# RWKV-6 attention and an MLP-mixer block on one core: unit 2's own gram moved into the state products' banks, its state products into mixing's banks, unit 3 started later

## The chip, the cores and the metric

The kernel runs on one core of a Trainium2 chip. The metric is the device time of one execution in microseconds; the median of three runs is 534.33 us (533.35 to 536.37). Five engines work beside each other and keep to their own order: TensorE (PE: matmuls, and PEld: its weight loads), VectorE (DVE), ScalarE (ACT), GpSimd (POOL) and SyncE (SP), which here issues nearly all DMAs. They wait for each other by semaphores.

## What is computed

Two blocks follow each other, in float32, for 4 batches, 768 tokens and 8 heads of 48:

```python
for t in range(S):                       # RWKV-6: a state of 48 x 48 per head
    cur = einsum('bhd,bhe->bhde', u * kt, vt)
    y[:, :, t] = einsum('bhd,bhde->bhe', rt, state + cur)
    state = wt[:, :, :, None] * state + einsum('bhd,bhe->bhde', kt, vt)
x = y.transpose(0, 2, 1, 3).reshape(B, S, H * D)
h = relu(x.T @ w_tok1) @ w_tok2          # mixing over tokens
u = x + h.T
out = u + relu(u @ w_ch1) @ w_ch2        # mixing over channels
```

The mixer's four weights come as 64-bit floats and are converted on the chip.

## The kernel before

**Units.** Attention is worked in units of 256 tokens of one batch: three to a batch, twelve in all. "Unit 0" to "unit 2" are the first batch, unit 3 is the first of the second batch. A unit has two blocks of 128 tokens and each of these two chunks of 64; within a chunk the recurrence becomes matmuls. `unit(i)` (L340) returns the steps of one unit as functions:

- `own_u` (four pieces): ScalarE multiplies the keys by u. `own_gram`: 64 small matmuls of these with the queries, `own_put`: VectorE puts their diagonal into the unit's attention matrix `at` (two of these, used in turn).
- `ends` and `begins`: VectorE scans the decays backwards and forwards; `keys` and `queries` multiply them in. `ranges`: two checks on ScalarE of the size of the decays.
- `tokens`: TensorE turns the keys; `copied`: two ScalarE copies of that out of PSUM into `kT`.
- `gram`, `mask`: keys by queries, and VectorE puts the part above the diagonal into `at`.
- `carry`: the products of keys and values that go into the state (`outer`, tile `kv_ps`). `updates`: state = scaled state + product, on VectorE. `scaled`: the state times the decay of a chunk, tile `before`; four ScalarE instructions for each chunk (L432), one for every pair of heads.
- `before`: the queries times the scaled states (`y_ps`, L311); `seen`: a small ScalarE copy that orders what follows; `after`: the attention matrix times the values (L332); `taken`: three ScalarE copies of the result to `x`.

**PSUM banks.** [...] `ps_a` has one tile of two banks, tag "a", for the state products. During the first batch `ps_g` has two tiles of two banks for grams and y, and `ps_m` has two single banks, tag "m", for turned keys and mixing. After the first batch `ps_g` and `ps_m` are closed and `ps_m` has six banks. A tile that takes a buffer waits until the last reader of the tile before it there is done.

**Weight conversions.** `convert` (L189) makes seven steps for each pair of weight pieces: a load by SP, then on VectorE L203 (exponent), L209 (mantissa), L215 (add), L218 (product) and two of L221 (put); on ScalarE L206 (power of two, needs L203) and L212 (sign). L218 needs both. Raw data lies in `scratch` and `spare` in turn. There are three for the token weights (`to_tok`) and nine for the channel weights (`to_ch`; in the text, conversion 0 to 8).

**Order.** `strict` (L88) fixes the order of instructions on TensorE, VectorE and ScalarE to that of the calls. For the first batch's attention the list is written by hand (L716 to L725), with the mixing of batch 0 (`h`) and the first conversions in it. From then on a list of (cost, step) pairs of the attention of the next batch (`steps`, L685) is woven by cost into the pieces of the mixing of the present batch (`woven`, L46). In mixing, `up` (L531) is three matmul instructions and a relu on ScalarE, `down` (L601) the second channel product. What stands in `ahead` (L765) is issued before any step of the next batch. A matmul instruction in float32 is recorded as two.

SP's order is the scheduler's, from the same calls; a load that waits holds those behind it.

## Time and profile before

| | us |
|---|---|
| median of the runs | 534.33 |
| profiled execution | 533.83 |
| its span | 532.0 |
| TensorE busy in the span | 504.4 |
| VectorE busy | 330.7 |
| ScalarE busy | 213.0 |
| PE idle before its first matmul | 8.52 |
| 64 small matmuls of a gram, slow clock / full clock | 1.98 / 1.16 |
| scan over a unit's decays (VectorE) | 2.33 |
| four scaled states of a chunk (ScalarE) | 1.01 |
| update of a state (VectorE) | 0.35 |

The span runs from the first instruction to the last; around it lie 1.83 us of the execution. In the lines of a profile, "x32" counts instructions as recorded, and a bracket names the time that the engine stood idle before a row and what it waited for.

### The profile page before, as it was taken

To read this page: it belongs to the slowest core of one execution; us is meant where nothing else is said; L and a number is where in the kernel's file an instruction comes from. 1 tells how busy PE (TensorE), PEld (TensorE's weight loads), DVE (VectorE), ACT (ScalarE), POOL (GpSimd) and SP (SyncE) were. 2 spreads that over 40 slices of the span, in tenths; PEclk is the share of its full clock that TensorE was granted. 3 is DMA by queue.
4 is the path that set the end of the run, shared out by engine and by line. 5 is a ranking of instruction groups with operands and counts; after the bars stand their busy time and mean duration, and the time that the engine had idled before them with its cause. 6 is when DMAs were issued, how large, how long until landed. Compare 5 with 4: busy or idle time off the path is not lost.

```text
span 532.0 us, 12569 instructions
## 1 busy us (share of the span) xinstructions
PE 504.4 (95%) x5506; PEld 430.1 (81%) x5506; DVE 330.7 (62%) x505; ACT 213.0 (40%) x533; POOL 1.3 (0%) x10
## 2 busy tenths in 40 slices
PE   3669989999999999999999999999999999999997
PEld 3567568766689868898998967898998968999996
DVE  7996899796195654193482665195393625775654
ACT  3857685772242234433343234423424303441400
POOL 0000000000000000000000000000000000000000
PEclk9688999999999999999999999999999999999999
DMA  8967747624222213214212203102000000000000
GB/s 300 331 174 216 225 157 244 190 91 125 95 71 90 91 34 97 60 36 126 60 71 91 64 27 102 31 1 91 1 31 1 3 30 1 1 0 32 1 33 32
DMA packets 20941, 46.01 MB, mean 86 GB/s; under 512 B 2128, under 2 KB 13008, under 8 KB 20880
## 3 DMA queue, kind: packets, MB, share of 16 engines
q1 hardware_dynamic: 20736, 45.14, 26.5%
q8 instruction: 45, 0.74, 0.6%
q14 instruction: 16, 0.13, 0.1%
q10 hardware_dynamic: 144, 0.00, 0.0%
HBM read 40.41 MB, written 4.72 MB: 85 GB/s over the span
## 4 chain that ended last, share of the span: by engine, by line
PE 82%; DVE 12%; ACT 3%; issue 2%; DMA 1%; DVEq 0%
PE q_ps L625 26%; PE z_ps L536 23%; PE h_ps L607 6%; PE z_ps L568 6%; PE h_ps L513 6%; PE h_ps L520 5%; PE y_ps L332 2%; PE y_ps L311 2%; PE kv_ps L297 2%; DVE to_end L366 2%; PE gram L251 2%; PE k_ps L281 1%; PE xT_ps L528 1%; DVE w L374 1%; DVE wch L221 1%
## 5 line engine op out<-in xcount | busy, mean ns | idle before, releaser
L536 PE MATMUL z_ps<-xT,wch 128*128 128x256 f32 x648 | 147.4, 382 | 1.0 <-DVE wch L221 1.0
L536 PEld LDWEIGHTS z_ps<-xT,wch 128*128 128x128 f32 x648 | 120.7, 190 | 17.9 <-DVE wch L221 1.4
L625 PE MATMUL q_ps<-wch,z 128*128 128x192 f32 x444 | 78.5, 328 | 0.0
L625 PEld LDWEIGHTS q_ps<-wch,z 128*128 128x128 f32 x444 | 72.6, 190 | 0.8 <-DVE z L667 0.3
L538 ACT ACTIVATE z<-z_ps 128x256 f32<-128x256 f32 x108 | 41.0, 382 | 79.5 <-PE z_ps L536 78.9
L432 ACT ACTIVATE before<-state,to_end 112x48 f32<-112x48 f32 x176 | 44.2, 324 | 30.3 <-DVE state L442 26.0
L625 PE MATMUL q_ps<-scratch,z 128*128 128x192 f32 x288 | 50.4, 328 | 0.0
L625 PEld LDWEIGHTS q_ps<-scratch,z 128*128 128x128 f32 x288 | 47.0, 190 | 0.3
L442 DVE TENSOR_TENSOR state<-before,kv_ps 112x192 f32<-112x192 f32 x40 | 13.9, 348 | 39.7 <-ACT before L432 31.4
L520 PE MATMUL h_ps<-h,wtok 128*128 128x384 f32 x96 | 34.9, 490 | 0.6 <-ACT h L515 0.6
L607 PE MATMUL h_ps<-wch,z 128*128 128x384 f32 x96 | 32.4, 490 | 0.0
L513 PE MATMUL h_ps<-x,wtok 128*128 128x384 f32 x96 | 32.1, 490 | 0.0
L635 DVE TENSOR_TENSOR o<-x,z 128x192 f32<-128x192 f32 x7 | 2.5, 358 | 45.3 <-ACT z L634 45.3
L522 DVE TENSOR_TENSOR x<-x,h_ps 128x384 f32<-128x384 f32 x24 | 13.3, 553 | 27.4 <-PE h_ps L520 27.3
L366 DVE TENSOR_TENSOR_SCAN to_end<-w,starts 112x1041 f32<-112x1041 f32 (+1 forms) x13 | 28.1, 2159 | 2.0 <-DMA w<-in_w_dram 1.6
L374 DVE TENSOR_TENSOR_SCAN w<-w,starts 112x1041 f32<-112x1041 f32 x12 | 27.9, 2321 | 0.0
L513 PEld LDWEIGHTS h_ps<-x,wtok 128*128 128x128 f32 x96 | 18.2, 192 | 11.6
L607 PEld LDWEIGHTS h_ps<-wch,z 128*128 128x128 f32 x96 | 17.8, 190 | 11.4
L338 ACT COPY x<-y_ps 64x384 f32<-64x384 f32 (+1 forms) x36 | 17.1, 475 | 22.0 <-PE y_ps L332 21.6
L520 PEld LDWEIGHTS h_ps<-h,wtok 128*128 128x128 f32 x96 | 16.6, 190 | 9.4 <-ACT h L515 2.3
L358 ACT ACTIVATE junk<-to_end,least 112x1041 uint8<-112x1041 f32 x12 | 13.9, 1162 | 25.5 <-DVE to_end L366 25.5
L529 ACT COPY xT<-xT_ps 128x384 f32<-128x384 f32 x24 | 11.4, 478 | 23.9 <-PE xT_ps L528 23.8
(140 smaller groups left out, 669.6 us busy)
## 6 DMA issues: line engine op xcount, KB each, us to landing
rk<-in_rk_dram SPq DMA_DIRECT2D x36, 192.0 KB, 3.6
near<-in_near_dram SPq DMA_DIRECT2D x8, 768.0 KB, 4.4
w<-in_w_dram SPq DMA_DIRECT2D x11, 520.5 KB, 3.7
spare<-in_w_ch_dram SPq DMA_DIRECT2D x10, 512.0 KB, 4.3
vt<-in_v_dram SPq DMA_DIRECT2D x12, 384.0 KB, 4.0
out_dram<-o SPq DMA_DIRECT2D x24, 192.0 KB, 1.9
scratch<-in_w_ch_dram SPq DMA_DIRECT2D x8, 512.0 KB, 4.2
rk<-in_rk_dram SPq DMA_DIRECT2D x6, 512.0 KB, 8.4
```

The lines of the kernel that those rows point to most:

```text
L338: return [lambda: act.copy(x[:, 0], got[0])] + [lambda n=n: act.copy(x[ts(n, P), 1], got[1][ts(1 - n, P)]) for n in range(2)]
L358: act.activation(junk[:ROWS], L["to_end"][:ROWS], AF.Relu, bias=bias[:ROWS], scale=scale, accum_out=flags[:ROWS, i, n:n + 1])
L366: dve.tensor_tensor_scan(to, of, start, 0.0, op0=ALU.mult, op1=ALU.add)
L374: dve.tensor_tensor_scan(w_[:ROWS], w_[:ROWS], starts[:ROWS], 0.0, op0=ALU.mult, op1=ALU.add)
L432: act.mul(t[:ROWS, a], state[bt, g][:ROWS, a], by_last(c, j)[:, a:a + 1])
L513: pe.matmul(sums[i], wtok1[:, c, ts(i, 128)], x_of()[:, c, :], start=(c == 0), stop=(c == C - 1))
L520: pe.matmul(ps, wtok2[:, i, ts(c, 128)], h1[:, i, :], start=(i == 0), stop=(i == DTOK // 128 - 1))
L536: pe.matmul(ps, wch1[:, m, ts(jt, 128)], xT[:, m, ts(s, SEG)], start=(m == 0), stop=(m == DM // 128 - 1))
L538: act.activation(zs[s][:, jt, :], ps, AF.Relu)
L568: pe.matmul(ps[:, q], lefts[r][:, ts(q, 128)], of[r], start=first and q == 0, stop=end and q == JB - 1, skip_group_check=True)
L607: pe.matmul(ps, zs[s][:, jt, ts(n, 128)], wch2[:, jt, :], start=(jt == 0), stop=(jt == NJ - 1))
L625: pe.matmul(ps, a[:, j, :], b[:, j, :], start=(j == 0), stop=(j == HJ - 1))
```

## The change

- `grams` takes an optional pool and tag. In unit 2 its own gram takes the two banks of `ps_a`, where the state products of unit 0 were, and not a tile of `ps_g`. In the order by hand it now comes before unit 0's `after`; `own_put` of unit 2 follows that of unit 1, ahead of unit 1's state products.
- `outer` takes `apart`. In unit 2 the products of even and odd chunks lie in two single banks of `ps_m` in place of the tile of `ps_a`.
- In unit 2 the last three `scaled` steps are one VectorE product each in place of four ScalarE instructions.
- The order by hand is changed accordingly: unit 2's `own_u`, `carry` and updates move, and four of the mixing's matmuls come behind unit 2's `before`.
- In unit 3 an empty step of cost 2.0 stands before `tokens`; and the first quarter of the pieces of batch 0's mixing after `ahead` (ups and conversions 2 and 3) is issued before any step of unit 3.

```diff
-    def grams(k_, r_):
+    def grams(k_, r_, where=None):
 
-        both = ps_g and ps_g.tile([128, 2, 512], f32, name="gram")
-        g = [both[:, q] for q in range(2)] if ps_g else [bank("gram") for q in range(2)]
+        where = where or (ps_g and (ps_g, "gram"))
+        both = where and where[0].tile([128, 2, 512], f32, name="gram", tag=where[1])
+        g = [both[:, q] for q in range(2)] if where else [bank("gram") for q in range(2)]
...
-    def outer(kT, vt, half):
+    def outer(kT, vt, half, apart=False):
 
-        kv = ps_a.tile([128, 2, 512], f32, name="kv_ps", tag="a")
+        both = None if apart else ps_a.tile([128, 2, 512], f32, name="kv_ps", tag="a")
+        kv = [bank("kv_ps") if apart else both[:, j] for j in range(2)]
...
         def own_gram():
-            L["own"] = grams(L.pop("uk"), r_)
+            L["own"] = grams(L.pop("uk"), r_, (ps_a, "a") if i == UB - 1 else None)
...
         def carry():
-            L["kv"] = outer(L.pop("kT"), vs[i], half)
+            L["kv"] = outer(L.pop("kT"), vs[i], half, apart=i == UB - 1)
...
                 t = L["before"][g] = apool.tile([128, A, D], f32, name="before", bufs=5)
+                if i == UB - 1 and (c, j) != (0, 0):
+                    return dve.tensor_mul(t[:ROWS], state[bt, g][:ROWS], by_last(c, j).unsqueeze(2).to_broadcast([ROWS, A, D]))
                 for a in range(A):
...
-                (2.4, e["ends"]), (1.2, e["keys"]), (0.4, e["ranges"][0]), (2.2, e["begins"]), (1.0, e["tokens"]), (0.2, e["copied"][0]),
+                (2.4, e["ends"]), (1.2, e["keys"]), (0.4, e["ranges"][0]), (2.2, e["begins"]),
+                *([] if by_tokens else [(2.0, lambda: None)]), (1.0, e["tokens"]), (0.2, e["copied"][0]),
...
-           x0, p0, s0[1], t0[2], m0, g0, e1["begins"], s0[2], t0[3], add0, s0[3], t1[0], e0["before"], e0["seen"], put0, load2,
-           e1["keys"], e0["after"], *e2["own_u"], e1["tokens"], *e1["copied"], e1["queries"], e1["own_put"], e1["carry"], *e0["taken"],
-           lambda: load_v(2), e1["gram"], e2["ends"], s1[0], t1[1], e2["keys"], e2["tokens"], s1[1], t1[2], e2["own_gram"], *e2["copied"],
-           e2["begins"], s1[2], t1[3], e1["mask"], s1[3], t2[0], e2["carry"], e1["before"], e2["queries"], s2[0], t2[1], e1["seen"],
-           e1["after"], e2["own_put"], e2["gram"], s2[1], t2[2], x1, e1["taken"][0], m1, *h[:2], s2[2], t2[3], e1["taken"][1], p1, e2["mask"],
-           e1["taken"][2], s2[3], e2["before"], e2["seen"], add1, g1, put1, to_ch[0][0], e2["after"], *h[2:8], x2, m2, *e2["taken"], p2,
-           add2, g2, *h[8:], put2,
+           x0, p0, s0[1], t0[2], m0, g0, e1["begins"], e2["own_u"][0], s0[2], t0[3], *e2["own_u"][1:], add0, s0[3], e0["before"], e0["seen"],
+           t1[0], e2["own_gram"], put0, load2, e1["keys"], e0["after"], e1["tokens"], *e1["copied"], e1["queries"], e1["own_put"],
+           e2["own_put"], e1["carry"], *e0["taken"], lambda: load_v(2), e1["gram"], e2["ends"], s1[0], t1[1], e2["keys"], e2["tokens"],
+           s1[1], t1[2], *e2["copied"], e2["carry"], e2["begins"], s1[2], t1[3], e1["mask"], s1[3], t2[0], e1["before"], e2["queries"],
+           e1["seen"], e1["after"], e2["gram"], x1, p1, s2[0], t2[1], s2[1], t2[2], s2[2], t2[3], *e1["taken"], s2[3], e2["before"], m1,
+           g1, e2["mask"], e2["seen"], *h[:2], e2["after"], add1, put1, to_ch[0][0], *h[2:8], *e2["taken"], x2, p2, m2, add2, g2, *h[8:], put2,
...
-            pieces = woven(both, sum(to_ch[2:8], [])) + woven(downs[0][:6], to_ch[8]) + downs[0][6:] + downs[1][:8]
+            pieces = woven(both, sum(to_ch[2:8], []))
+            alone = len(pieces) // 4
+            ahead += pieces[:alone]
+            pieces = pieces[alone:] + woven(downs[0][:6], to_ch[8]) + downs[0][6:] + downs[1][:8]
```

In the list, e0 to e2 are the units' steps, s their updates, t their scaled states, and x, m, p, add, g, put the steps of the token weights' conversions. In the built program this gives, on TensorE, 36 matmul instructions of `up` before unit 3's turned keys where 15 stood; on VectorE, conversions 2 and 3 as a whole before unit 3's `ends`; and on SP, the load of `near` and of `u_rows` later among the loads of conversions 5 to 8, in front of conversion 8's.

More of the change, by code (lines that the diff above doesn't have):

```diff
@@ L253, in grams @@
                 start=True, stop=True))
-        if ps_g:
+        if where:
             return [(slice(0, 2), both.rearrange("p q (x t) -> p q x t", x=X))]
@@ L296, in outer @@
                     if 2 * (half * UC + c) + j < 2 * C - 1:
-                        pe.matmul(kv[ts(q, P), j, ds((c * A + a) * D, D)], kT[ts(j, T), c, a, ts(q, P)],
+                        pe.matmul(kv[j][ts(q, P), ds((c * A + a) * D, D)], kT[ts(j, T), c, a, ts(q, P)],
                                   vt[ts(j, T), c, ts(2 * a + q, D)], start=True, stop=True)
@@ L437, in update @@
                 new = state[bt, g + 1] = apool.tile([128, A, D], f32, name="state", bufs=3)
-                got = L["kv"][:ROWS, j, ds(c * A * D, A * D)].rearrange("p (a e) -> p a e", a=A)
+                got = L["kv"][j][:ROWS, ds(c * A * D, A * D)].rearrange("p (a e) -> p a e", a=A)
                 if g == 0:
@@ L838, in by_halves @@
                         new = states[g + 1] = apool.tile([128, A, D], f32, name="before", bufs=5)
-                        got = kv[:ROWS, j, ds(c * A * D, A * D)].rearrange("p (a e) -> p a e", a=A)
+                        got = kv[j][:ROWS, ds(c * A * D, A * D)].rearrange("p (a e) -> p a e", a=A)
                         if g == 0:
```

## The prediction

> **What bounds the kernel now.** I read the page first: busy shares, then the forty slices (13.3 us each).

> ```profile
> PE 504.4 (95%) x5506; PEld 430.1 (81%) x5506; DVE 330.7 (62%) x505; ACT 213.0 (40%) x533; POOL 1.3 (0%) x10
> ...
> PE   3669989999999999999999999999999999999997
> ...
> PEclk9688999999999999999999999999999999999999
> ```

> TensorE is full from the eighth slice on, with a low clock only in the second to fourth. Then busy time by stretch (second column length, third TensorE, then weight loads, VectorE, ScalarE):

> ```profile
> 9.00:110.00 101.00, 85.96 (x1469) 69.28 (x1463) 88.15 (x120) 71.45 (x162) 0.00 (x0) 0.92 0.72 232
> 110.00:200.00 90.00, 90.00 (x894) 66.09 (x893) 56.46 (x73) 30.33 (x80) 0.00 (x0) 1.00 0.24 76
> ```

> TensorE idles 101.00 - 85.96 = 15.04 us between 9 and 110 us, and next to nothing afterwards until the end. The change touches only the work before 140 us and removes no matmul. So the new time is the old one, less idle or slow-clock time removed, plus idle time added, all before about 120 us. The list of waits says what TensorE stood for:

> ```profile
> PE y_ps L311 <- ACT before L432: 2.7, 2, 1.4
> PE gram L251 <- issue: 2.0, 1, 2.0
> PE kv_ps L297 <- DVE state L442: 2.0, 1, 2.0
> PE k_ps L281 <- issue: 2.0, 1, 2.0
> PE y_ps L332 <- ACT seen L320: 1.6, 3, 1.0
> ...
> PE k_ps L281 <- DVE rk L371: 1.0, 1, 1.0
> ```

> The change aims at the 2.0 of kv (at 36.86 us), the 1.0 of k_ps (76.21) and half of the 2.7 of y (1.30 at 99.89). The k_ps "issue" ends at 32.69, just when VectorE's keys of unit 2 end (31.38 + 1.21), so it is really a wait for VectorE. Last, ScalarE's and VectorE's timelines at 70 us, which carry my forecast:

> ```profile
> 71.40 0.38 ACT L538 ACTIVATE z<-z_ps 128x256 f32<-128x256 f32 x1
> 71.68 1.14 ACT L206 ACTIVATE scratch<-scratch,rebias 128x1024 uint16<-128x1024 uint16 x1
> 72.72 1.16 ACT L358 ACTIVATE junk<-to_end,least 112x1041 uint8<-112x1041 f32 x1
> ...
> 73.87 1.17 ACT L212 ACTIVATE scratch<-spare 128x1024 bf16<-128x1024 int32 x1
> ```

> ```profile
> 70.60 2.33 DVE L366 TENSOR_TENSOR_SCAN to_end<-w,starts 112x1041 f32<-112x1041 f32 x1
> ...
> 74.94 1.22 DVE L371 TENSOR_TENSOR rk<-rk,to_end 112x1024 f32<-112x1024 f32 x1
> 76.07 0.68 DVE L218 TENSOR_TENSOR scratch<-scratch 128x1024 bf16<-128x1024 bf16 x1
> ```

> A weight conversion needs ScalarE twice (L206, L212) before VectorE can go on (L218). Unit 3's scan and keys now fill VectorE while ScalarE does that. The change moves exactly this filling away.

> [...] a gram of 64 matmuls takes 1.98 us at 8.52 and 1.16 us at 78.53, and the changes between slow and fast lie near 14.6, 28.2 and 45.3 us. [...] I price the new 112x192 products by L442's 0.35 us of the same size.

> **The change part by part, units 0 to 2.** Times are those of the profiled execution; I follow the built order of the changed program on each engine and what each wait names.
> - Unit 0's y ends at 23.34 (22.21 + 1.13). Unit 2's own gram now follows. Its four scaled keys (4 in 1.70 us) come one before and three behind the third scaled state, which ends at 22.84, so the last is ready at about 24.1; 40 of 64 matmuls remain, at 1.98/64 each 1.2 us: end 25.3. "seen" is ready at 24.2 as before, so within starts at 25.3 instead of 24.36: +0.95.
> - Unit 2's own_put (1.13 us pitch) goes ahead of its scan on VectorE. The gram sat in the state products' banks, so unit 1's kv waits for that: 28.5 + 1.15 = 29.7 instead of 28.13. Behind it wait unit 1's gram and updates; those wait for the same scan anyway. Keys of unit 2 end at 33.7 instead of 32.6.
> - k_ps then ends at 34.8, ScalarE's two copies at 36.05, and unit 2's kv starts at once in mixing's banks; with the old banks it would wait for unit 1's last update at 37.9.
> - Unit 1's "seen" comes behind the first scaled state of unit 2 (37.9 to 38.9): within starts at 39.15 (before 40.78).
> - Unit 2's updates and three products on VectorE take 6 x 0.35 after 39.65: done at 41.85 instead of ScalarE's 44.1. Each product replaces four ScalarE instructions of 0.32.
> - Unit 2's y then waits only for unit 1's results to be taken (1.45 us of copies): with a full clock it ends at 43.3, four matmuls of the mixing at 44.65, within at 45.8. With the slow clock kept until 45.3 (within 1.96, gram 1.95) within ends at 48.1.
> Before, the twenty mixing matmuls that follow start at 48.78. So the gain is 0.75 to 3.0; I take S = 1.8, since 31.7 to 35.1 is still half idle and the slow clock likely comes back.

> **Units 3 on.** Here I keep the clock of before and subtract S at the end, as the whole loop from 50 to 70 us is unchanged and moves along. TensorE now does twelve ups (36 matmul instructions) before k_ps instead of five: an up is 6 recorded matmuls of 0.2265 (5.45/24), 1.36 us. The second ends at 71.15, the twelfth at 84.75.
> - Conversion 2: VectorE is ready at 72.3, but L206, the range check and L212 run 71.68 to 74.9. It ends at 76.9 (0.72 + 1.21).
> - Conversion 3: L203 to 77.5, L206 to 78.55, now the scaled keys of unit 3 (1.6) and one relu (0.3), L212 to 81.55; end 83.5. VectorE stood idle about 2.6 + 2.2 us.
> - Only then unit 3's scan (2.64 with reciprocal) and keys (1.13): 87.3. k_ps waits 84.75 to 87.3: 2.55.
> - Its own gram needs the bank of up 10, whose relu stands behind the next L206 and L212: 87.3 + 0.6 + 1.05 + 0.3 + 1.05 + 0.3 = 90.6; TensorE is there at 89.7: 0.9. A later up waits 0.2 the same way.
> - Scaled-state chain: conversion 5 and own_put end at 97.6, queries 100.7, first update 103.4, ScalarE product to 104.35, L212 to 105.4, conversion 6 to 107.35, mask to 111.3, third update 111.65, L206 and L212 before the third scaled state: 112.55 to 113.5.
> - TensorE has done its 24 ups by 109.0; y waits 1.1 for a bank and then about 2.2 for that state; it ends at 113.9.
> Before, y ended at 100.89 after 54 instructions; 18 more make 18 x 2 x 0.2265 = 8.15, so 109.05. The loss is 113.9 - 109.05 = 4.85 (waits of 7.0 for the 2.26 of before). The last conversion ends at 123.9 and is needed at 125.75, so nothing more is late, and later units have slack.
> SP: unit 4's near load, u_rows and an rk load now stand between the conversions' loads. u_rows waits for own_put (97.6), so half of conversion 7's load goes out at 98.1 and, at 4.2 us, lands before its use at 107.4. Free; if late, up to 2 us.

> **The sum.** -1.8 + 4.85 = +3.05 on the profiled execution's 533.83 (span 532.0 and 1.83 around it): 536.9. The runs' median is 0.5 above that execution, so I put 537.4 for the median.

> **Rivals.**
> - Faster: the fourth unit costs nothing, because the conversions run ahead in the free quarter as they are meant to and leave the 0.96 and 1.30 waits behind. For it: VectorE saves 3.8 us of scan and keys there. Against: ScalarE is 9.19 of 10 busy at 66 to 76 us. 534.33 - 1.8 - 2.26 = 530.3. It decides if conversion 3 ends before 81, so that keys are ready by 84.75.
> - No change: the clock stays full (S = 3.0) and the later chain costs 3: 534.3.
> - Clearly slower: no early gain, as kv's new wait for own_put and a slow clock eat it all (S near 0), and SP's order makes a load 1 us late: 540.
> - The change might not do what it says if kv still waited; in the built order it waits for ScalarE's key copies alone, so I give this no weight of its own.

> **How the numbers follow.** Forecast 0.50 (own range 535.8 to 539), faster 0.17, no change 0.20, clearly slower 0.13. Under 0.5% (2.7 us, about what can be told here) lies the bottom of the forecast's range, 0.14 of its 0.50. So slower 0.36 + 0.13 = 0.49, same 0.20 + 0.14 = 0.34, faster 0.17. The range 531 to 540 leaves out most of the faster case and the end of the slow one, some 0.2.

> **What would show it.** Right: kv of unit 2 with no wait for state; the mixing's first long run of matmuls some 2 us earlier; VectorE waiting for L212 twice near 70 to 80 us; TensorE waiting over 2 us before unit 3's k_ps and again at its y. Wrong: no k_ps wait near 85 us, or low clock all through 30 to 50 us.

## The result and the profile after

The changed kernel takes 543.48 us (median of 5 runs, 541.88 to 544.21), the kernel before 534.33 (median of 5, 533.25 to 536.37): a ratio of 1.0163, 95% interval 1.0131 to 1.0194. The profiled execution has a span of 541.8 us against 532.0. The change makes the kernel slower, as forecast, but by 9 us and not by 3.

The page of the changed kernel, in the rows shown of before:

```profile
PE 511.1 (94%) x5506; PEld 434.4 (80%) x5506; DVE 331.8 (61%) x508; ACT 210.1 (39%) x521; POOL 1.3 (0%) x10
...
PE   3679987989999999999999999999999999999997
...
PEclk9676998979999999999999999999999999999999
```

TensorE has the same 5506 matmul records, yet is busy 511.1 us and not 504.4. The last row says why: the granted clock is lower than before in the third and fourth slice (7 and 6 tenths, where it was 8 and 8) and again in the seventh and ninth (8 and 7). In these two the PE row has new dents as well. Busy time by stretch (the columns are those shown of before):

```profile
9.00:110.00 101.00, 85.53 (x1353) 69.05 (x1346) 84.04 (x116) 61.85 (x131) 0.00 (x0) 0.86 0.67 215
110.00:200.00 90.00, 87.52 (x908) 64.19 (x906) 56.32 (x73) 34.19 (x93) 0.00 (x0) 0.96 0.29 89
```

In the first stretch TensorE is busy as long as before, with 116 fewer matmuls and a mean clock of 0.86 where it was 0.92. In the second, which was free of idle time and of slow clock, it now has both. What TensorE waited for (us in all, times, longest):

```profile
PE y_ps L313 <- ACT before L436: 3.7, 2, 1.9
PE k_ps L282 <- ACT junk L360: 3.3, 1, 3.3
PE k_ps L282 <- issue: 1.9, 1, 1.9
...
PE kv_ps L299 <- ACT kT L283: 1.4, 2, 0.7
...
PE y_ps L313 <- ACT z L542: 0.6, 1, 0.6
```

The wait of kv for an update (2.0 before) is gone, as intended. In its place stand 3.3 us before unit 3's turned keys and more time at its y. The row names ScalarE's range check, but that ended earlier; VectorE's keys end at 89.10 and the transposes start at 89.20. Its timeline shows why these are so late:

```profile
72.74 1.23 DVE L215 SCALAR_TENSOR_TENSOR scratch<-spare,scratch 128x1024 f32<-128x1024 uint32 x1
76.59 0.69 DVE L218 TENSOR_TENSOR scratch<-scratch 128x1024 bf16<-128x1024 bf16 x1 [2.62 <-ACT scratch L212]
...
83.31 0.69 DVE L218 TENSOR_TENSOR scratch<-scratch 128x1024 bf16<-128x1024 bf16 x1 [2.23 <-ACT scratch L212]
...
85.40 2.33 DVE L368 TENSOR_TENSOR_SCAN to_end<-w,starts 112x1041 f32<-112x1041 f32 x1
...
87.94 1.16 DVE L373 TENSOR_TENSOR rk<-rk,to_end 112x1024 f32<-112x1024 f32 x1
```

VectorE stands twice, 2.62 and 2.23 us, for ScalarE's sign step of a conversion, and only then scans unit 3's decays, which lay in just such a wait before. TensorE's timeline at unit 3's keys and y (start, duration, count, and in brackets the idle time ahead):

```profile
89.20 1.06 PE L282 MATMUL k_ps<-ident,rk 128*128 128x128 f32 x8 [3.30 <-ACT junk L360]
90.10 2.45 PE L540 MATMUL z_ps<-xT,wch 128*128 128x256 f32 x6
92.48 1.76 PE L252 MATMUL gram<-rk,near 48*64 48x64 f32 x64
...
112.10 0.66 PE L313 MATMUL y_ps<-before,rk 48*64 48x48 f32 x18 [0.62 <-ACT z L542]
114.63 1.12 PE L313 MATMUL y_ps<-before,rk 48*64 48x48 f32 x28 [1.87 <-ACT before L436]
115.69 5.49 PE L611 MATMUL h_ps<-wch,z 128*128 128x384 f32 x8
```

After each wait the granted clock falls to 0.50 (from 90.4 to 93.8 us and from 114.3 to 121.1): six records of z take 2.45 us, where six take 1.46 at full clock, and the eight of h 5.49 where they take 2.85. And TensorE in the part where the first batch should have gained:

```profile
38.51 2.00 PE L313 MATMUL y_ps<-before,rk 48*64 48x48 f32 x57
40.76 1.96 PE L334 MATMUL y_ps<-vt,at 64*64 64x48 f32 x64 [0.25 <-ACT seen L322]
42.50 1.95 PE L252 MATMUL gram<-rk 48*64 48x64 f32 x64
44.29 2.10 PE L313 MATMUL y_ps<-before,rk 48*64 48x48 f32 x64
46.32 2.93 PE L517 MATMUL h_ps<-x,wtok 128*128 128x384 f32 x4
49.18 1.25 PE L334 MATMUL y_ps<-vt,at 64*64 64x48 f32 x64
```

Everything from 38 to 49 us runs at half clock (granted 0.50 from 35.8 to 49.5), 1.95 for a gram of 64 in place of 1.16. The run of twenty mixing matmuls that follows starts at 50.36; before, at 48.78.

The 9.8 us of the span: 1.58 in the first batch (50.36 - 48.78); 5.1 up to the end of unit 3's y (115.75, against 100.89 + 8.15 for the eighteen instructions that now stand ahead of it, + 1.58 = 110.62); 2.6 in the slow matmuls behind it (5.49 - 2.85). That is 9.3; the other 0.5 I didn't trace.

### The profile page after: what moved, and what is told of

Its sections match the earlier page's. It is cut to its first block, busy times and chain, and to the rows that moved or that the text cites. A ratio compares the mean times of both kernels' runs of the same rounds, so it can differ in the third digit from the quotient of the medians.

```text
span 541.8 us, 12559 instructions
## 1 busy us (share of the span) xinstructions
PE 511.1 (94%) x5506; PEld 434.4 (80%) x5506; DVE 331.8 (61%) x508; ACT 210.1 (39%) x521; POOL 1.3 (0%) x10
## 4 chain that ended last, share of the span: by engine, by line
PE 81%; DVE 9%; DMA 4%; ACT 4%; issue 2%; SPq 1%; DVEq 0%; ACTq 0%
PE q_ps L629 26%; PE z_ps L540 21%; PE h_ps L611 6%; PE h_ps L517 6%; PE z_ps L572 6%; PE h_ps L524 5%; PE y_ps L313 2%; PE y_ps L334 2%; DMA w<-in_w_dram 2%; PE kv_ps L299 2%; PE gram L252 2%; DMA rk<-in_rk_dram 2%; PE k_ps L282 1%; PE xT_ps L532 1%; DVE wch L221 1%
## 5 line engine op out<-in xcount | busy, mean ns | idle before, releaser
L436 ACT ACTIVATE before<-state,to_end 112x48 f32<-112x48 f32 x164 | 41.2, 324 | 24.7 <-DVE state L446 23.3
L629 PEld LDWEIGHTS q_ps<-scratch,z 128*128 128x128 f32 x288 | 47.1, 190 | 0.2
L611 PE MATMUL h_ps<-wch,z 128*128 128x384 f32 x96 | 35.1, 522 | 0.0
L517 PE MATMUL h_ps<-x,wtok 128*128 128x384 f32 x96 | 33.4, 504 | 0.0
L526 DVE TENSOR_TENSOR x<-x,h_ps 128x384 f32<-128x384 f32 x24 | 13.3, 553 | 28.5 <-PE h_ps L524 28.3
L639 DVE TENSOR_TENSOR o<-x,z 128x192 f32<-128x192 f32 x7 | 2.5, 358 | 44.9 <-ACT z L638 44.9
L313 PEld LDWEIGHTS y_ps<-before,rk 48*64 48x64 f32 x704 | 16.0, 157 | 7.5 <-ACT before L436 4.0
```

The costliest lines, as they stand in the source:

```text
L313: pe.matmul(y[q][put(q, j), ds((c * A + a) * D, D)], r_[q * P:q * P + D, ds((c * A + a) * 128 + j * T, T)], before[g][q * P:q * P + D, a, ...
L436: act.mul(t[:ROWS, a], state[bt, g][:ROWS, a], by_last(c, j)[:, a:a + 1])
L517: pe.matmul(sums[i], wtok1[:, c, ts(i, 128)], x_of()[:, c, :], start=(c == 0), stop=(c == C - 1))
L611: pe.matmul(ps, zs[s][:, jt, ts(n, 128)], wch2[:, jt, :], start=(jt == 0), stop=(jt == NJ - 1))
L629: pe.matmul(ps, a[:, j, :], b[:, j, :], start=(j == 0), stop=(j == HJ - 1))
```

## The experiments

The runs of one group share the chip with runs of the kernel before (medians 534.47 to 535.15); a ratio is to these. One profiled execution stands behind each time of an event, and it need not be a typical one, since the executions of a kernel differ in how often the clock falls. For each execution the mean granted clock is on record. With a granted clock of 0.50 in stretches of 3.41 us (both measured, see the last section) it gives the number of slow stretches: (1 - 0.984) x 2 x 532.0 / 3.41 = 5 for the profiled execution of the kernel before. In 58 executions of that kernel it is 4 to 8, on average 6.0; the eleven with 5 have a median of 533.54 us, the ten with 7 of 536.53.

### Which half costs: the parts alone

**first_batch_only.** The free quarter and the empty step are taken back; the new first batch stays.

```diff
-                *([] if by_tokens else [(2.0, lambda: None)]), (1.0, e["tokens"]), ...
+                (1.0, e["tokens"]), ...
-            alone = len(pieces) // 4
-            ahead += pieces[:alone]
```

> The first batch's part alone (unit 2's own gram, banks, VectorE products, order by hand); unit 3 starts as before. Theory A (the first batch loses only what the profile shows there, 1.6 us, because the slow clock lasts until 49 us; the late start of unit 3 is worth 5 us of waits and some 3 us of slow clock behind them): about 1.6 us over the kernel before, 535 to 537. Theory B (the early order is the whole loss, by the wait for unit 2's own_put and what follows it; the late start is free): 542 to 544. Theory C (the two parts only cost something together): within 1 us of before.

Measured: 535.38 (20 runs), ratio 1.0006, 0.9991 to 1.0021. The new first batch shows neither a gain nor a loss, and theories A and C both allow this time. A gain of 1.8 us (0.9966) lies outside of the interval. On average its executions have 7.25 slow stretches, those of the kernel before beside them 6.05.

**fourth_later_only.** The kernel before with the empty step and the free quarter alone.

> Unit 3 later alone (empty step and free quarter), the first batch as before. Theory A: the waits of the walk, 4.85 us, and some 3 us of slow clock after them: 541 to 543, with waits of TensorE over 2 us before unit 3's turned keys and at its y. Theory B: 534 or below. Theory C: within 1 us of before.

Measured: 541.22 (4 runs), ratio 1.0144, 1.0086 to 1.0202. The same 3.30 us before unit 3's keys, and slow matmuls behind it (z of six 2.77). So by the medians 6.6 us of the 9 come from the later fourth unit, as theory A said; the interval reaches from 4.6 to 10.8. The two parts add up to 7.3 over their runs of before; the remainder is of the size of the intervals.

**no_empty_step** and **no_free_quarter** split the later part, with the new first batch left in.

> The change without the empty step of cost 2.0 (the free quarter of mixing stays). My theory: the free quarter is what costs, since it takes unit 3's scan out of VectorE's wait for ScalarE; the empty step alone only moves turned keys by two ups. So a k_ps wait of 2.5 to 4 us near 85 us stays and the time is 541 to 544 us, within 2 us of the changed kernel's 543.5. Rival (the empty step matters, because it pushes unit 3's state chain back): 538 or less.

> The change without the free quarter (the empty step stays). My theory: unit 3's scan fills VectorE as before, there is no k_ps wait over 0.5 us, y waits as before (1.3 to 1.5 us), and the time is 534.5 to 536.5 us, like the kernel with the new first batch alone (535.4). Rival (the empty step matters): 538 us or more with a y wait over 2.5 us.

Measured: 541.63 (4 runs; 1.0103, 1.0057 to 1.0148) without the empty step, with a wait of 5.20 before the keys (2.5 to 4 was expected); 535.09 (20 runs; 1.0002, 0.9987 to 1.0018) without the free quarter, with none. The free quarter is what costs. The empty step does no harm that can be told. What the theory missed: TensorE's timeline without the free quarter has the last part of unit 3's y nearly without a wait (1.45 in first_batch_only):

```profile
102.51 0.99 PE L313 MATMUL y_ps<-before,rk 48*64 48x48 f32 x28 [0.24 <-ACT before L436]
```

**before_empty_step** puts that one step into the kernel before.

> The kernel before with the empty step of cost 2.0 alone. In the change without the free quarter, unit 3's y waited 0.24 us where it waited 1.3 to 1.5 us without the empty step. Theory (the empty step is the useful part of the change, as it gives unit 3's states more matmuls to be made behind): no wait over 0.5 us at y, and a time of 533.0 to 534.0 us, about 1 us under the kernel before. Rival (what is won at y is lost at the next waits, as unit 4 comes later): 534.2 to 535.5 us.

Measured: 533.86 (14 runs), ratio 0.9984, 0.9966 to 1.0002; unit 3's y waits 0.24. The time is where the theory put it, but the interval reaches 1, so a gain isn't shown. The rival's wait is there too, before unit 4's turned keys, where the kernel before has none:

```profile
115.66 1.06 PE L281 MATMUL k_ps<-ident,rk 128*128 128x128 f32 x8 [1.33 <-ACT junk L358]
```

It has the lowest median of the kernels tried.

### Why the later fourth unit costs: VectorE's order, and the clock behind each wait

**keys_ahead.** The whole change, with seven steps of unit 3 (a load, its scaled keys, `ends`, `keys`) woven into the free quarter. TensorE's order is that of the changed kernel.

```diff
-            ahead += pieces[:alone]
+            free, early = pieces[:alone], 7
...
         att = [e for i in range(n, n + UB) if i < NU for e in steps(i)]
+        if bt == 0:
+            ahead += woven(att[:early], free)
+            att = [(c, lambda: None) for c, _ in att[:early]] + att[early:]
```

> The change with unit 3's scaled keys, scan and keys issued among the free quarter's conversions; TensorE's order is that of the changed kernel. My theory (VectorE and not TensorE's own order makes unit 3 late: the scan is no longer in the waits for the sign of a conversion): VectorE no longer idles 2.2 to 2.6 us there, the k_ps wait of 3.3 goes to under 0.5, the slow clock behind it goes, all later waits of unit 3 shrink by 2 us or more, and the time is 535.5 to 538 us. Rival (the state chain is late for its own length, whatever the keys do): y still waits 3 us or more and the time stays above 540 us.

Measured: 537.82 (20 runs), ratio 1.0053, 1.0037 to 1.0069. VectorE's timeline in that kernel:

```profile
75.20 2.33 DVE L368 TENSOR_TENSOR_SCAN to_end<-w,starts 112x1041 f32<-112x1041 f32 x1
...
79.33 0.69 DVE L218 TENSOR_TENSOR scratch<-scratch 128x1024 bf16<-128x1024 bf16 x1 [1.51 <-ACT scratch L212]
...
82.47 1.22 DVE L373 TENSOR_TENSOR rk<-rk,to_end 112x1024 f32<-112x1024 f32 x1
...
84.74 0.68 DVE L218 TENSOR_TENSOR scratch<-scratch 128x1024 bf16<-128x1024 bf16 x1
```

The scan lies in the first wait for the sign again, the keys fill the second, and they are done 5.4 us earlier on the clock of this execution (82.47 + 1.22 against 89.10). TensorE no longer waits for unit 3's keys, and 5.7 of the 9 us are back. So it is the order on VectorE, not that TensorE takes up unit 3 later, that costs most. What the theory missed: y still waits 0.63 for a bank and 1.87 for a scaled state, as in the changed kernel. Those waits do hang on the length of the state chain, as the rival said, though they didn't hold the time above 540. The clock falls behind them again (the eight h matmuls after y take 4.28 in the profiled execution, at 540.05 us the longest of the twenty).

**after_fill.** The changed kernel with unread transposes of the identity on TensorE, 24 before unit 3's turned keys and 12 before its y.

```diff
+        for m in range(warm):
+            pe.transpose(both[m // A % UC][:, m % A, :], ident, ident)
```

> The changed kernel with unread transposes of the identity in TensorE's two late waits: 24 before unit 3's turned keys (3.2 us), 12 before its y (1.6 us). Theory A (the waits bring the slow clock, which costs the run of the second channel product after y 2.8 us: 5.49 for 8 matmuls in place of 2.7): those 8 matmuls take about 2.7 and the kernel is 2 to 3.5 us faster than the changed one, 540 to 541.5, though TensorE has 4.8 us more to do. Rival (the slow clock there has another cause, or the fill only delays): 543 or more.

Measured: 541.11 (4 runs), ratio 1.0123, 1.0089 to 1.0157. The same stretch of TensorE:

```profile
90.10 1.46 PE L544 MATMUL z_ps<-xT,wch 128*128 128x256 f32 x6
...
114.65 0.99 PE L317 MATMUL y_ps<-before,rk 48*64 48x48 f32 x28 [1.72 <-ACT before L440]
115.57 2.85 PE L615 MATMUL h_ps<-wch,z 128*128 128x384 f32 x8
```

y ends where it did (115.64 against 115.75), as its data come no earlier, but the eight h matmuls take 2.85 and not 5.49. That is 2.6 us in the trace: the price of the slow clock which the waits brought. The medians are 2.4 apart, but with 5 and 4 runs the two intervals overlap.

### Why the first batch gains nothing

**before_warm2.** The kernel before with 12 unread transposes in the wait of 2.0 before unit 2's turned keys.

> The kernel before, with 12 transposes of the identity (nobody reads them) in front of unit 2's turned keys, where TensorE waits 2.0 us for VectorE's keys: 1.6 us of full-size work at full clock. Theory A (the slow clock from 35 to 45 us comes from the idle time before it): the clock stays full, unit 1's within and unit 2's gram take 1.15 each in place of 1.95, and the kernel is 1 to 3 us faster than before, 531 to 533.5. Rival (the clock falls because these matmuls are small, or for reasons outside of this wait): no change, 534 to 535.

Measured: 534.17 (20 runs), ratio 1.0003, 0.9984 to 1.0022: no change, as the rival said. In the profiled execution the clock fell all the same and stayed low until 48 us; a second gap of 1.91 us, before unit 2's state products, was still there. That execution is one of the slowest (537.27 us, 8 slow stretches). On average there are 6.2, against 6.05 in the kernel before: filling this one gap didn't keep the clock up.

**first_filled.** first_batch_only with transposes in three gaps: 8 before unit 1's state products, 13 before unit 2's turned keys, 5 before its state products.

> The new first batch alone (no free quarter, no empty step), with 26 unread transposes of the identity on TensorE: 8 before unit 1's state products, 13 before unit 2's turned keys, 5 before unit 2's state products, each in a gap in which it waits. My theory of the early part (the gain of 1.8 is lost to the slow clock that the gaps from 28 to 37 us bring): the 64 matmuls of y, within and gram at 38 to 45 us take 1.2 us each and not 1.96, the run of mixing matmuls starts near 46 us and not 48.4, and the time is 532.5 to 533.5 us. Rival (the clock falls for another cause, such as the small matmuls themselves, or on its own beat): these take 1.9 us or more and the time stays at 535 to 536 us.

Measured: 536.37 (22 runs), ratio 1.0043, 1.0024 to 1.0063. TensorE's timeline:

```profile
39.08 1.15 PE L317 MATMUL y_ps<-before,rk 48*64 48x48 f32 x58
40.55 1.15 PE L338 MATMUL y_ps<-vt,at 64*64 64x48 f32 x64 [0.32 <-ACT seen L326]
...
43.71 0.33 PE L317 MATMUL y_ps<-before,rk 48*64 48x48 f32 x8 [1.07 <-ACT x L344]
44.83 1.03 PE L317 MATMUL y_ps<-before,rk 48*64 48x48 f32 x56 [0.78 <-issue]
...
48.36 1.24 PE L521 MATMUL h_ps<-x,wtok 128*128 128x384 f32 x3
```

The clock held, as the theory said, and the time did not fall. TensorE, faster, now stands 1.07 us for ScalarE's copies of unit 1's result and 0.78 at "issue" (see the last section), and the mixing's run starts at 48.36, as in first_batch_only (48.35). Part of that is of the experiment's own making: the first eight transposes waited for the state products' banks and put off unit 1's first update from 32.39 to 33.67.

**refilled, one_gap_filled, gaps_filled** were to mend that: no_free_quarter with 13 transposes before unit 2's keys and 4 before its state products; with the 13 alone; and with 22 that were put into banks which the next steps take anyway.

> The change without the free quarter (its first batch and the empty step stay), with 17 unread transposes of the identity on TensorE: 13 before unit 2's turned keys and 4 before its state products; unit 1's state products have none in front of them this time. My theory (the run with 26 held the clock up but paid for it, since the 8 in front of unit 1's products put off that unit's states and keys by 1.4 us): the matmuls at 38 to 45 us take 1.2 us, the run of mixing matmuls starts at 46 to 47.2 us, and the time is 533.0 to 534.2 us, 1 to 2 us under the same kernel without them (535.1). Rival (the early path is set by VectorE and ScalarE, whatever the clock): the run starts at 48 us or later and the time stays at 535 us or more.

> As the run beside it, but with the 13 transposes before unit 2's turned keys only; the gap of 0.5 to 0.7 us before its state products stays. In the kernel before, filling the one gap didn't hold the clock up, but there a second gap of 2.0 us followed. Theory (what counts is how much of a stretch TensorE stands): with only short gaps left the clock stays full in most runs, and the time is within 0.7 us of the other run, 533.0 to 534.5 us. Rival (any gap there brings the slow clock): matmuls of 1.9 us at 38 to 43 us, and 535 us or more.

> The change without the free quarter, with 22 unread transposes of the identity on TensorE that wait for nothing the next step doesn't have anyway: 5 before unit 1's state products (into the banks that its gram takes next), 13 before unit 2's turned keys, 4 before unit 2's state products (into the banks that unit 1's y takes next). Theory (the early gain is there and the slow clock alone eats it; the runs before put off the state products by the place of their transposes): unit 2's state products start by 36 us, the 64 matmuls of y, within and gram at 37 to 43 us take 1.2 us each, the run of mixing matmuls starts at 46.3 to 47.3 us, and the time is 533.0 to 534.2 us. Rival (with a full clock TensorE waits for ScalarE's copies of unit 1's result and for VectorE instead): the run starts at 48 us or later and the time is 535 us or more.

Measured: 536.58 (22 runs; 1.0030, 1.0013 to 1.0047), 535.42 (14 runs; 1.0008, 0.9988 to 1.0028) and 536.65 (22 runs; 1.0020, 1.0004 to 1.0037), against 535.09 without transposes. All three miss their theory. In the profiled executions the clock fell later, at about 39 us, but stayed low to 50 us or more, and gaps_filled stood 3 us at another place. Over all executions, though, the clock isn't what makes these kernels slow: first_filled, refilled and one_gap_filled have 5.5, 5.5 and 5.6 slow stretches on average, against 6.65 in no_free_quarter. The six executions of refilled with at most 4 take 533.99 to 535.69 us; the five with 4 of the kernel before beside them have a median of 532.57. So with the transposes in, a fuller clock wins nothing, which speaks for the rivals (waits of TensorE other than for the clock) or for a price of the transposes themselves. What it would bring without them isn't settled.

**mixing_earlier and before_mixing_later.** The profiled executions gave another lead. Where the first four mixing matmuls came behind unit 2's y, as the change has them, the slow clock ended at 49.3 us or later in all but first_batch_only and first_filled; with these four in front, by 48.1. Two kernels move these four alone: no_free_quarter with them back in front of unit 2's y, and the kernel before with them behind it.

```diff
-           e1["seen"], e1["after"], e2["gram"], ..., s2[3], e2["before"], m1,
-           g1, e2["mask"], e2["seen"], *h[:2], e2["after"], ...
+           e1["seen"], e1["after"], e2["gram"], ..., s2[3], *h[:2], e2["before"], m1,
+           g1, e2["mask"], e2["seen"], e2["after"], ...
```

> The change without the free quarter, with the first four of the mixing's matmuls put back in front of unit 2's y on TensorE, as they stood in the kernel before; nothing else moves. Theory (the slow stretch near 36 to 50 us ends late because the order now has unit 2's y ahead of these matmuls, so that a further stretch of clock time holds only matmuls of 48 by 48 and short gaps): the slow stretch is 7 to 10 us long and not 13.7, it ends by 46 us, the run of mixing matmuls starts by 48.8 us, and the time is 533.2 to 534.5 us against 535.1. Rival (the place of these four says nothing; the length of the slow stretch follows from gaps alone): it stays at 10 to 14 us and the time at 534.8 to 536 us.

> The kernel before, with the first four of the mixing's matmuls moved behind unit 2's y and in front of its attention times values, as the change has them; nothing else moves. Theory (as beside it): the slow stretch from 38 us grows from 6.8 to 10 us or more and the time to 535.2 to 537 us. Rival: it stays at 6.8 us and the time within 0.5 us of the kernel before.

Measured: 534.30 (22 runs), ratio 0.9996, 0.9982 to 1.0010; and 537.35 (22 runs), ratio 1.0040, 1.0025 to 1.0056. In before_mixing_later:

```profile
41.35 1.95 PE L251 MATMUL gram<-rk 48*64 48x64 f32 x64
45.10 1.15 PE L311 MATMUL y_ps<-before,rk 48*64 48x48 f32 x64 [1.80 <-ACT x L338]
46.18 2.58 PE L513 MATMUL h_ps<-x,wtok 128*128 128x384 f32 x4
48.70 1.71 PE L332 MATMUL y_ps<-vt,at 64*64 64x48 f32 x64
50.34 4.14 PE L513 MATMUL h_ps<-x,wtok 128*128 128x384 f32 x12
```

With nothing in between, y stands 1.80 us for ScalarE's copies, where it stood 0.16 before, and a further piece of slow clock follows (h of four 2.58). This edit of the order costs 2 to 3 us in the old first batch, measured alone (0.40%, with an interval of 1.3 to 3.0 us; the medians are 2.8 apart). Over all executions it brings 7.6 slow stretches on average in place of 6.2. In mixing_earlier:

```profile
44.72 1.59 PE L517 MATMUL h_ps<-x,wtok 128*128 128x384 f32 x4
46.24 1.15 PE L313 MATMUL y_ps<-before,rk 48*64 48x48 f32 x64
...
48.75 5.43 PE L517 MATMUL h_ps<-x,wtok 128*128 128x384 f32 x16
```

Here the slow clock ends by 45 us and the run starts at 48.75, within 0.03 us of before. Against 535.09 with the four behind y it may have won 0.8, but the intervals overlap. That the first batch then reaches the old time and no more is shown; a gain isn't. Nor is the theory's mechanism: the slow stretch of this execution is 10.2 us and not 7 to 10, and over all executions there are 6.64 slow stretches with the four in front and 6.65 with them behind. So what before_mixing_later shows for the old first batch doesn't carry over to the new one. Slow clock between 30 and 53 us, from the clock changes in the trace of each profiled execution, and the start of the mixing's run, by the place of the four matmuls:

| four matmuls | kernel | slow clock, us | run starts |
|---|---|---|---|
| in front of y | before | 37.9 to 44.8 | 48.78 |
| | before_empty_step | 38.5 to 45.4 | 48.30 |
| | fourth_later_only | 38.7 to 45.6 | 48.45 |
| | mixing_earlier | 34.6 to 44.8 | 48.75 |
| behind y | changed | 35.8 to 49.5 | 50.36 |
| | first_batch_only | 34.7 to 44.9 | 48.35 |
| | no_free_quarter | 36.0 to 49.6 | 50.58 |
| | no_empty_step | 35.9 to 49.5 | 50.35 |
| | keys_ahead | 34.4 to 51.4 | 51.54 |
| | after_fill | 35.7 to 49.3 | 50.37 |
| | before_mixing_later | 32.9 to 36.3, 39.7 to 43.2, 46.6 to 50.0 | 50.34 |
| with transposes, in front | before_warm2 | 37.8 to 48.1 | 50.67 |
| with transposes, behind | first_filled | 30.1 to 33.6 | 48.36 |
| | refilled | 39.7 to 50.0 | 50.80 |
| | one_gap_filled | 38.4 to 52.1 | 51.41 |
| | gaps_filled | 39.2 to 52.9 | 52.71 |

## Why the prediction was wrong

The direction and the course of unit 3 were right, the size wasn't: 537.4 was predicted, 543.48 measured, above the range. Two terms failed: S, a gain of 1.8 us that didn't come, and the slow clock behind the new waits, which stood at nothing and cost 2.6. By its steps:

- **Unit 3's chain, priced at 4.85.** Right: 5.1. VectorE's idle times were predicted as 2.6 and 2.2 and are 2.62 and 2.23; keys ready at 87.3 in the times of before, measured 89.10 - 1.58 = 87.5; the wait before the keys 2.55 against 3.30; at y 1.1 and 2.2 against 0.62 and 1.87; y's end 113.9 against 115.75 - 1.58 = 114.2. keys_ahead shows the cause of the wait before the keys. The waits of 0.9 at unit 3's own gram and 0.2 behind it didn't come; slow matmuls took 1.6 us there instead (z 2.45 - 1.46, gram 1.76 - 1.16). The sum doesn't feel it, since the end of y hangs on the chain of states.
- **What follows y: the term that was left out.** The sum said that after y "nothing more is late" and went on at full clock. But behind the new waits on TensorE the granted clock fell to 0.50, at 90.4 and at 114.3 us. After the first (z at 2.45, gram at 1.76) the loss hid itself in the waits further on; after those at y there was nothing left to hide it: 2.6 us, shown by the trace of after_fill. The prediction reckoned with a slow clock in the first batch ("the slow clock likely comes back"), and not behind the waits that it added itself.
- **S, the early gain, taken as 1.8 out of 0.75 to 3.0: the step that failed most.** In the profiled execution it is -1.58, a miss of 3.4; over the medians of first_batch_only there is no gain (535.38 against 534.65). The engines' side was right: unit 2's state products start at 35.69 (predicted 36.05) without the wait for an update, and VectorE's last product ends at 42.21 (41.85). TensorE's side was wrong. The low end rested on "the slow clock kept until 45.3", read from the kernel before, and on a full clock with no other wait for the high end. In the changed kernel the slow clock lasted to 49.5: half of these 4.2 us is 2.1, of the 2.3 us between the low end and the measured -1.58. In first_batch_only, where it ended at 44.9, the run started at 48.35, close to the 48.1 of the low end. The executions as a whole fit with that: no_free_quarter has 6.65 slow stretches on average against 6.0, and with six of them takes 533.40 us against 534.45, with seven 535.48 against 536.53. Where the clock is alike, then, about 1 us is won (with the empty step in it). This compares small groups whose stretches may lie at different places, so it is a hint and no proof.
- **TensorE's other waits there, counted in part.** At full clock (first_filled) y has waits that the sum gave only in part: 1.07 for copies that ScalarE starts behind a conversion step, 0.78 at "issue". The second ends 1.3 to 1.4 us after a packet on the instruction queue landed (last section), and the sum has no term for it. The records behind it come no earlier in the kernels without transposes: 44.83 us in first_filled, 45.28 in the changed kernel, 45.18 in first_batch_only. That may be why first_filled, at full clock from 33.6 on, starts the run no earlier than first_batch_only: 48.36 and 48.35, a gain of 0.4. On VectorE the new products took 0.36 us each, where 0.35 was priced.
- **Slips in the sums.** They are small: 39.65 + 6 x 0.35 is 41.75 and not 41.85, 5.45/24 is 0.227, the low end 48.78 - 48.1 is 0.7 and not 0.75, and the waits of 7.0 less 2.26 make 4.7 where the ends of y give 4.85.
- **The order by hand.** Moving four full-size matmuls behind unit 2's y was priced as neutral. before_mixing_later shows 2 to 3 us for it in the old first batch: the matmuls had covered y's wait for copies. In the new first batch such a cost isn't shown (mixing_earlier).
- **The rivals.** "Clearly slower" had one of its two mechanisms right, no early gain through the slow clock; of the late load on SP nothing shows in the waits. Of the signs named for the main story three came true (unit 2's state products without a wait for a state, VectorE idle twice, the waits of unit 3, at y 2.5 us in two parts); the mixing's run 2 us earlier didn't. Of those against it the low clock came, though from 35.8 to 49.5 and not all through 30 to 50.

Open is what the new first batch would bring with a full clock. first_filled starts its run at 48.36 with unit 1's update 1.3 us late; an estimate from these two numbers gives about 47.1 without the delay, near the predicted 47. But it leaves out the gap at "issue", which needn't come earlier then; no run got there. When the clock returns in the new first batch isn't settled either: with the same order on TensorE it was at 44.9 in first_batch_only and at 49.6 in no_free_quarter.

## What to carry to other kernels

Before steps are moved to give one engine a lead, look at what lies inside the waits of another: here the scan and keys of a unit stood in VectorE's waits for ScalarE, and moving them out cost more than the lead was worth. Price a new wait on TensorE twice, once for itself and once for the slow clock that may follow (2.6 us here, behind unit 3's y), and look whether a later wait still hides the second. A gain in a stretch of small matmuls and short gaps isn't safe until its clock is known over several executions; the mean granted clock of each execution says whether the profiled one is typical.

## What the runs showed of the hardware

**In different kernels TensorE stands at the same counts of its records.** In the changed kernel, inside unit 2's state products:

```profile
35.69 1.16 PE L299 MATMUL kv_ps<-vt,kT 64*64 64x48 f32 x18 [0.71 <-ACT kT L283]
37.29 1.21 PE L299 MATMUL kv_ps<-vt,kT 64*64 64x48 f32 x26 [0.44 <-issue]
```

The gap after eighteen of them is there in the kernel before too. In one_gap_filled, with 13 transposes ahead, it comes after 2 + 3 = 5:

```profile
35.61 0.31 PE L301 MATMUL kv_ps<-vt,kT 64*64 64x48 f32 x2 [0.72 <-ACT kT L285]
36.09 0.31 PE L301 MATMUL kv_ps<-vt,kT 64*64 64x48 f32 x3 [0.17 <-ACT kT L285]
37.19 0.96 PE L301 MATMUL kv_ps<-vt,kT 64*64 64x48 f32 x40 [0.79 <-issue]
```

With 12 ahead (before_warm2) it comes after 6, with 17 (refilled) after 2, and with 22 (gaps_filled) in front of them all, in the weight loads of the last four transposes:

```profile
34.75 0.14 PEld L428 LDWEIGHTS y_ps<-ident 128*128 128x128 f32 x1
37.92 0.36 PEld L428 LDWEIGHTS y_ps<-ident 128*128 128x128 f32 x3 [3.02 <-issue]
```

The place moves by about one for every matmul put in front, so it belongs to the stream of instructions and not to the data. Counted over all of TensorE's records in a trace (weight loads, matmuls and semaphores), it doesn't move at all: 1217 records stand ahead of the gap in each of the eleven traces that have it. In the kernel before, a gap of 2.03 us at "issue" lies inside a gram near 18 us:

```profile
18.48 1.44 PE L251 MATMUL gram<-rk,near 48*64 48x64 f32 x42 [2.03 <-issue]
```

All sixteen traces have it, each with 449 records ahead; a third one, near 45 us in six of them, has 1729. The page counts 45 packets of 0.74 MB on a queue for instructions, about 16 KB each:

```profile
q8 instruction: 45, 0.74, 0.6%
```

Each of the three gaps ends 1.3 to 1.7 us after the first, fourth and sixth packet landed: the second one in the changed kernel at 37.29 after 35.81, in gaps_filled at 37.92 after 36.30. In no trace does one of the three records behind them come earlier than 1.28 us after its packet, gap or no gap. The third lies in unit 2's y. In the changed kernel it comes at 45.28, in first_batch_only at 45.18, in first_filled at 44.83, each 1.3 to 1.4 us after its packet. By these times I estimate that y, with these packets, could hardly have gone on earlier, whatever the clock. Whether the packets come earlier when TensorE is ahead wasn't tried.

By these times I read the gaps as waits for such a packet; that is an estimate, since no run moved the transfers themselves. TensorE stands 0.2 to 3.0 us in the second gap, in a stretch where 64 matmuls take 1.15 us.
